# Strided convolution with group norm and GELU, forward and backward: stores of the input gradient in two halves, the first block's leaf C by halves of channels, and a new order for the G1 stage

## The chip, the cores and the metric

One core of a Trainium2 chip runs the whole program in one launch. The metric is the device time of the program in microseconds (us). PE is the matrix engine, PEld its loading of weights, DVE the vector engine, ACT the scalar engine, POOL the general engine, and SP the queue that issues nearly all transfers.

## The reference

```
x [2, 16000, 256], w [31, 256, 256], gn_gamma [256], gn_beta [256], grad_out [2, 7985, 256], all bf16

def _fwd_reference(x, w, gn_gamma, gn_beta):
    s = 2; L = (T - K) // s + 1                       # 7985
    h = sum over i < 31 of einsum('blc,cd->bld', x[:, i:i + s*L:s, :], w[i])
    mu, var = mean and variance of h over l
    h = (h - mu) / sqrt(var + 1e-5) * gn_gamma + gn_beta
    return gelu(h, approximate=True)

def reference(x, w, gn_gamma, gn_beta, grad_out):
    out, vjp = jax.vjp(_fwd_reference, x, w, gn_gamma, gn_beta)
    return out, *vjp(grad_out)                        # out, dx, dw, dgamma, dbeta
```

It is a convolution of stride 2 with 31 taps over 16000 rows of 256 channels, a normalisation of each channel over the rows, and GELU; then the gradients of all four inputs. The kernel returns them as out_0 to out_4; out_1 is the input gradient.

## The kernel before, in words

The three convolutions (forward, input gradient, weight gradient) are fast convolutions in the manner of Karatsuba, nested over the phases of rows and taps. At each of two levels a product of two-part operands is replaced by three products of A (one part), C_ (the other part) and B_ (their sums or differences). A third level is used where `three` or `outer` says so: `f_three_b` computes the product of the sums with difference weights WD or W2D, ACT copies it inside PSUM into the places where it is needed (L778, L1357), and `f_three_ac` adds the other two. The plain form of the same leaf is `f_leaf`: for each of two halves dh of the output channels, it runs over four tap positions q, two parities par and two halves ch of the input channels; an even q is one matmul of 512 columns, an odd q two of 256.

The stages are F0 (forward, batch item 0), F1 (forward, item 1, with GELU of item 0 beside it), G0 (input gradient, blocks 0 to 2 of item 0), G1 (input gradient from block 3 of item 0 to the end) and W (weight gradient). An input gradient block c has two parts pr, each with the three branches B_, A, C_ and their three leaves.

`f_first` (L966) is the very first forward block. It makes the transformed weights on DVE with `w_sub` (L684): W[B_] as W[C_] - W[A] by halves of channels, W[.][B_], and the difference weights WD. Its three leaves are A (plain, in three pieces, so that it can begin with what is loaded), then C_ and B_ by the three-product form, with their own sums `third` (L700). `keep` (L837) takes the B_ leaf out of PSUM when the block is done.

In the input gradient, `e_load` (L1197) fetches two arrays (dy and h) for each half dh of a block, `e_comp` (L1205) turns them into the gradient ahead of the normalisation (L1212, L1214, L1223; on DVE for the blocks in EDVE, on ACT for the others, the last addition always on DVE) and spreads it into the tile ET. From block 0 of item 1 on, both halves share one buffer. `g_sums` builds the sums `first`, `second`, `third` from it (L1283). `g_seed` (L1391) starts the accumulators of two leaves, `g_evac` (L1401) adds a finished leaf to the B_ branch's result and writes it to the tile HO; with the last leaf of a part, it stores HO, the finished block of rows of out_1. There is one HO: the next part writes it again when the store has read it. `dl_turn` transposes the leaves with transfers for the weight gradient.

The order of all instructions is written out by a planner in the kernel itself (`Plan`, L39). Each operation is recorded with its engine, an assumed duration and what it depends on; a kind is made of the stage, the function and its caller (`"G1 load e_load"`). A due time comes from the PE work recorded so far, followed back through the successors:

```
due[i] = end - full - self.lead.get(o["kind"], 0.0) - self.fine.get(o["kind"], {}).get(o["part"], 0.0)
```

`lead` (L53 on) is an offset for a kind, `fine` one for a kind in a part, the number of the block; a larger offset makes the operation due earlier. `listing` (L335) then walks through an assumed run and gives each free engine the ready operation that is due first; PE may look 13 operations ahead. A transfer, and what depends on a transfer, counts as ready later the later it is due. On the chip each engine executes its instructions strictly in the order that comes out.

Of the kernel before, what the change touches and what calls it, by code (L numbers as in the profile page):

```python
# [20 lines left out]
A, B_, C_ = 0, 1, 2  # L21
# [9 lines left out]
def act(n, extra=0.0):  # L31
    return 0.06 + n * 0.00097 + extra
# [6 lines left out]
class Plan:  # L39
# [3 lines left out]
    def __init__(self, tc):  # L43
# [68 lines left out]
            "G0 turn gelu_batch": -12.0,  # L112
            "G0 w_sum load_w2": -53.0,
            "G0 w_sum w2_outer": -11.5,
            "G1 cp e_comp": 13.5,
            "G1 e_comp e_load": 13.5,
            "G1 g_evac last": -0.5,
            "G1 g_mm g_outer": -7.5,
            "G1 g_mm g_three_ac": -9.0,
            "G1 g_mm g_three_b": -30.5,  # L120
            "G1 g_three_b input_grad": -66.0,
            "G1 keep g_seed": -132.0,
            "G1 load dl_turn": 11.0,
            "G1 load e_load": -8.0,
            "G1 load g_evac": 12.0,
            "G1 spread e_comp": -1.5,
            "G1 tt first": -1.0,
            "G1 tt second": -17.0,
            "G1 tt third": -86.5,
            "G1 turn dl_turn": 3.5,  # L130
            "G1 zero e_comp": -8.0,
            "W keep w_keep": -3.0,
            "W keep weight_grad": -12.5,
            "W leaf_d weight_grad": 0.5,
# [83 lines left out]
            "G0 turn dl_turn": {0: -1.0, 1: -2.0, 2: -3.0},  # L218
            "G0 turn gelu_batch": {1: -84.5, 5: -72.0},
            "G0 w_sum load_w2": {3: 79.0},  # L220
            "G1 cp e_comp": {1: 17.0, 2: -24.5},
            "G1 e_comp e_load": {0: 33.5, 2: 1.5, 3: 0.5},
            "G1 g_evac last": {2: 6.5, 3: 5.0},
            "G1 g_mm g_outer": {1: -18.5, 2: -6.0, 3: -2.5},
            "G1 g_mm g_three_ac": {0: -75.0, 1: -51.0, 2: 8.5, 3: -1.5},
            "G1 g_mm g_three_b": {1: -16.5, 2: 16.5, 3: 21.0},
            "G1 g_seed input_grad": {1: -64.5, 2: 8.5, 3: 6.5},
            "G1 keep g_evac": {1: -1.5, 2: -8.0, 3: -5.5},
            "G1 load dl_turn": {0: -3.5, 1: -1.5, 2: 3.5},
            "G1 load e_load": {0: -112.0, 1: -15.0, 2: -56.0, 3: 1.0},  # L230
            "G1 load g_evac": {1: -23.0, 3: -26.0},
            "G1 spread e_comp": {0: -92.5, 1: -85.5, 2: -11.0, 3: -5.5},
            "G1 tt first": {3: -5.0},
            "G1 tt second": {0: -34.0, 1: 7.0, 2: 14.0, 3: 6.0},
            "G1 tt third": {3: 86.5},
            "G1 turn dl_turn": {0: 0.5, 1: 1.5, 2: 0.5, 3: 1.0},
            "G1 zero e_comp": {2: 20.0, 3: 23.0},
            "W keep w_keep": {0: 2.5, 3: -11.5, 4: 11.0, 5: 6.5, 6: -13.0},
            "W keep weight_grad": {0: 7.0, 1: 1.5, 2: -4.0, 3: -2.0, 4: 23.5},
            "W leaf_d weight_grad": {0: 1.5, 1: -14.5, 2: -49.5, 3: 27.0, 4: -0.5, 5: -6.5, 6: -16.0, 7: 12.5, 8: -21.0},  # L240
# [230 lines left out]
def conv_stem_kernel(  # L471
# [20 lines left out]
    HM = 256  # L492
# [32 lines left out]
    def sb(off, *shape, dt=BF16):  # L525
        n = int(np.prod(shape)) * (2 if dt == FP32 else 1)
        assert off % 32 == 0 and off + 2 * n <= AR, (off, shape)
        v = arena[:, off // 2:off // 2 + n]
        if dt == FP32:
            v = v.bitcast(FP32)  # L530
        if len(shape) == 1:
            return v
        names = "abcdefg"[:len(shape)]
        return v.rearrange("p (" + " ".join(names) + ") -> p " + " ".join(names), **dict(zip(names, shape)))
# [7 lines left out]
    def load(out, in_, nbytes, run, eng="SP", slack=None, own=False):  # L542
        if plan.stage in ONE and nbytes > 4096 and not own:
            eng = "SP"
        e = {"SP": nc.sync, "POOL": nc.gpsimd, "ACT": nc.scalar}[eng]
        pk = 8192 if run >= 4096 else 4096 if eng == "POOL" else run
        np_ = nbytes / pk
        ns = (PKS if out.space == bass.MemoryType.DRAM else PK)[pk]
        add(eng, {"POOL": 0.74, "SP": 0.46 + 0.00016 * np_, "ACT": 0.4}[eng], [out], [in_],
            lambda: e.dma_start(out=out, in_=in_), dma=np_ * ns / 16e3 * 1.03, ns=ns, tp=SH[pk], slack=slack)  # L550
# [19 lines left out]
    U = [sb(o, 2, F) for o in (138240, 142592, 205312)]  # L570
# [119 lines left out]
    def i_tap(q, par, br, lf):  # L690
        return 8 * q + par + 4 * (lf == C_) + 2 * (br == C_)
# [70 lines left out]
    def f_three_b(ps, br, lf, op, co, we):  # L762


        jobs = []
        for dh in range(2):
            for q2 in range(2):
                for par in range(2):
                    for ch in range(2):
                        o0 = (2 * par + ch) * XM + co + q2  # L770
                        n = we if q2 + par + ch else HM
                        jobs.append((0, slice(HM * dh, HM * dh + n), WD[br, lf][:, ch, q2, par, dh * P:(dh + 1) * P],
                                     op[:, 1, o0:o0 + n], dh + q2 + par + ch == 0))
        f_mm(ps, jobs, [ps[:, 0]], [WD[br, lf], op[:, 1]])
        for o, i, sc in ((ps[:, 1, 0:HM], ps[:, 0, HM:512], 1.0), (ps[:, 1, HM:512], ps[:, 0, HM:512], -1.0),
                         (ps[:, 0, HM:512], ps[:, 0, 0:HM], -1.0)):
            add("ACT", act(256), [o], [i],
                lambda o=o, i=i, sc=sc: nc.scalar.activation(out=o, in_=i, func=ACT.Copy, scale=sc))  # L778

    def f_three_ac(ps, br, lf, u, co, we, wo):  # L780
        for half, ua, ww in ((0, u[:, 0], we), (1, u[:, 1], wo)):
            for dh in range(2):
                jobs = []
                for q2 in range(2):
                    for par in range(2):
                        for ch in range(2):
                            q = 2 * q2 + half
                            if i_tap(q, par, br, lf) < K:
                                o0 = (2 * par + ch) * XM + co + q2
                                jobs.append((dh, slice(HM * half, HM * half + ww),  # L790
                                             W[br][:, lf, ch, q, par, dh * P:(dh + 1) * P], ua[:, o0:o0 + ww], False))
                f_mm(ps, jobs, [ps[:, dh]], [W[br][:, lf], ua, ps[:, dh]])
# [25 lines left out]
    def flat2(ps):  # L818
        return ps[:].rearrange("p a f -> p (a f)")
# [146 lines left out]
    def f_first(xt):  # L966
        for sl in (A, C_):
            for ch in range(2):
                for v in ([slice(None)] if ch or sl == C_ else [0, 1]):
                    w_sub(*(W[br][:, sl, ch, :, v] for br in (B_, C_, A)))  # L970
        ops, third, second = f_sums(xt, 0, 0, B_, 0, [W[B_][:, A, 0, :, v] for v in range(2)])
        second(A)
        second(C_)
        for br in (B_, A, C_):
            for ch in range(2):
                w_sub(W[br][:, B_, ch], W[br][:, C_, ch], W[br][:, A, ch])
            v = W[br][:, B_]
            w_sub(WD[br, B_], v[:, :, 1:4:2], v[:, :, 0:4:2])
        for br in (A, C_, B_):
            for lf in (A, C_):  # L980
                v = W[br][:, lf]
                w_sub(WD[br, lf], v[:, :, 1:4:2], v[:, :, 0:4:2])
        third(C_, U[2])
        third(B_, U[1])
        pa, pc, pb = ring[0], ring[1], ring[3]
        f_leaf(pa, B_, A, ops[A], 0, HM, HM, True, (0,), (0,))
        f_leaf(pa, B_, A, ops[A], 0, HM, HM, False, (0,), (1,))
        f_leaf(pa, B_, A, ops[A], 0, HM, HM, False, (1,))
        for ps, lf, u in ((pc, C_, U[2]), (pb, B_, U[1])):
            f_three_b(ps, B_, lf, ops[lf], 0, HM)  # L990
            f_three_ac(ps, B_, lf, u, 0, HM, HM)
        tb = TS[A].rearrange("p d f -> p (d f)")
        keep(tb, flat2(pb))
        ve(RB[:, 0], flat2(pa), tb, ALU.add)
        ve(RB[:, 1], flat2(pc), tb, ALU.subtract)
# [397 lines left out]
    def g_evac(b, c, pr, br, lf, ps):  # L1393
        if br == B_:
            keep(GRB[:, 0 if lf == A else 1].rearrange("p e f -> p (e f)"), flat2(ps))
            return
        ho = HO[pr % len(HO)]
        k = (0 if br == A else 1) + (0 if lf == A else 2)
        g = GRB[:, 0 if lf == A else 1]
        add("DVE", dve(1024, 1), [ho[:, :, k, :]], [ps[:], g],  # L1400
            lambda: nc.vector.tensor_tensor(out=ho[:, :, k, :], in0=ps[:], in1=g, op=ALU.add))  # L1401
        if br == C_ and lf == C_:
            n0 = 512 * c + 256 * pr
            r = P if c < 3 or pr == 0 else 104
            load(out_1[b, 8 * n0:8 * n0 + 16 * r, :].rearrange("(p r) c -> p (r c)", r=16),
                 ho[0:r].rearrange("p e k f -> p (e k f)"), r * 8192, 4096, "POOL", slack=60.0)

    G3 = {(b, br, B_) for b in range(NB) for br in ORDER}
    GO = {(b, c) for b, c in ((0, 3), (1, 0), (1, 1), (1, 2), (1, 3))}
# [456 lines left out]
```

## Time and profile before

| | |
|---|---|
| median of 3 runs | 1148.43 us (1147.74 to 1150.5) |
| the profiled execution | 1148.4 us, span 1146.6 us |
| PE busy | 1117.3 us, 97% |
| DVE busy | 998.8 us, 87% |
| ACT, POOL busy | 532.4 us, 124.4 us |
| moved by DMA | 243.57 MB, mean 212 GB/s |
| PE idle ahead of the forward's matmuls (L742) | 12.6 us |
| PE idle ahead of the input gradient's (L1330) | 9.5 us |

In the rows of the profile a group of instructions has its line, engine, operation, output <- input, and the number of executions; then the busy time, the mean duration in ns, and the idle time of the engine ahead of it with what ended it. In a timeline a row has the start, the duration, the engine, the line, the operation, and in brackets the idle time ahead of it. In a table of windows a row has the stretch, its length, the busy time of each engine (PE, PEld, DVE, ACT, POOL) with its instructions, the clock that was granted to PE, the share of DMA and GB/s. In the list of waits: who waited for what, us in total, times, the longest.

### The profile page before, as it was taken

How to read it: one execution, taken by the hardware profiler on the slowest of the kernel's cores; microseconds unless marked ns; L12 is line 12 of the kernel's file. 1: busy time of each engine (PE TensorE's matmuls, PEld its weight loads, DVE VectorE, ACT ScalarE, POOL GpSimd, SP SyncE). 2: the span in 40 equal slices, each digit the busy share in tenths (PEclk: the TensorE clock that was granted, in tenths of full speed). 3: DMA queues.
4: the chain of work that ended last, by engine and by line, in shares of the span. 5: the costliest groups of instructions: out<-in, count | busy, mean ns of one | idle time of the engine just before them, and what ended most of it. 6: DMA issues, size and time to landing. Idle time of an engine off the chain costs nothing. (4 is left out here: it accounts for less than half of the span.)

```text
span 1146.6 us, 18837 instructions
## 1 busy us (share of the span) xinstructions
PE 1117.3 (97%) x7598; PEld 749.3 (65%) x7652; DVE 998.8 (87%) x932; ACT 532.4 (46%) x817; POOL 124.4 (11%) x221
## 2 busy tenths in 40 slices
PE   5999999999999999999999899999999999999998
PEld 3888899877777884444444444444488766666785
DVE  7997787798989998998999777976799998788995
ACT  1254453768777488987744255633212212111200
POOL 0000000000000002231233133232200000000000
PEclk8999999999999999999999999999999999999999
DMA  9476658678895699999989688886998815999564
GB/s 220 66 175 138 164 139 172 147 189 192 193 222 132 192 363 277 280 259 277 229 224 218 136 214 190 205 214 163 247 334 267 291 64 200 350 333 308 185 199 128
DMA packets 345999, 243.57 MB, mean 212 GB/s; under 512 B 233569, under 2 KB 317159, under 8 KB 341735
## 3 DMA queue, kind: packets, MB, share of 16 engines
q1 hardware_dynamic: 338807, 223.47, 73.4%
q0 software_dynamic: 7104, 18.89, 5.8%
q8 instruction: 60, 0.98, 0.4%
q14 instruction: 28, 0.23, 0.1%
HBM read 106.24 MB, written 80.25 MB: 163 GB/s over the span
## 5 line engine op out<-in xcount | busy, mean ns | idle before, releaser
L742 PE MATMUL ps<-arena 128*128 128x256 bf16 (+4 forms) x3460 | 408.4, 282 | 12.6 <-DMA arena<-in_x_dram 6.0
L1330 PE MATMUL ps<-arena 128*128 128x512 bf16 (+1 forms) x1833 | 401.6, 377 | 9.5 <-DVE arena L1283 3.3
L742 PEld LDWEIGHTS <-arena 128*128 128x128 bf16 x3460 | 339.1, 99 | 81.7 <-DMA arena<-in_x_dram 6.3
L1330 PEld LDWEIGHTS <-arena 128*128 128x128 bf16 x1872 | 183.6, 98 | 226.3 <-issue 10.2
L1537 PE MATMUL ps<-arena 128*128 128x256 bf16 (+1 forms) x2305 | 308.3, 296 | 3.4 <-DVE arena L1703 1.8
L1537 PEld LDWEIGHTS <-arena 128*128 128x128 bf16 x2320 | 226.7, 98 | 85.1 <-DVE arena L1607 1.9
L837 ACT ACTIVATE arena<-ps 128x1024 f32<-128x1024 f32 x109 | 110.8, 1021 | 253.1 <-PE ps L1537 82.7
L700 DVE TENSOR_TENSOR arena<-arena 128x2080 bf16<-128x2080 bf16 (+8 forms) x126 | 156.5, 1266 | 34.4 <-PE ps L742 33.8
L550 POOL DMA_DIRECT2D dld<-arena x144 | 104.3, 727 | 259.7 <-DMA arena<-arena 247.3
L1117 DVE TENSOR_TENSOR arena<-arena 128x2048 bf16<-128x2048 bf16 (+1 forms) x80 | 95.6, 1195 | 9.1 <-ACT arena L1109 4.9
L1283 DVE TENSOR_TENSOR arena<-arena 128x1032 bf16<-128x1032 bf16 (+1 forms) x126 | 87.4, 725 | 8.1 <-ACT arena L1232 4.8
L1502 DVE TENSOR_TENSOR arena<-arena 128x4096 bf16<-128x4096 bf16 (+1 forms) x50 | 87.1, 1773 | 5.9 <-DMA arena<-in_x_dram 5.7
L1391 DVE TENSOR_TENSOR ps<-ps,arena 128x2048 f32<-128x2048 f32 x30 | 68.9, 2297 | 24.9 <-PE ps L1330 13.8
L1401 DVE TENSOR_TENSOR arena<-ps,arena 128x1024 bf16<-128x1024 f32 x64 | 77.0, 1218 | 8.0 <-PE ps L1330 5.3
L857 ACT ACTIVATE arena<-ps 128x512 bf16<-128x512 f32 (+1 forms) x64 | 37.1, 581 | 54.0 <-PE ps L742 53.5
L1639 ACT COPY ps<-ps 128x256 f32<-128x256 f32 x54 | 19.3, 358 | 84.2 <-PE ps L1537 82.5
L559 POOL MEMSET arena<- 128x128 bf16 (+11 forms) x40 | 8.6, 245 | 428.3 <-DVE arena L700 139.9
L1357 ACT COPY ps<-ps 128x512 f32<-128x512 f32 x48 | 27.7, 577 | 48.6 <-PE ps L1330 48.4
L1708 DVE TENSOR_TENSOR arena<-arena 128x4608 bf16<-128x4608 bf16 x16 | 40.6, 2551 | 4.7 <-PE ps L1537 4.7
L812 ACT ACTIVATE arena<-ps 128x512 f32<-128x512 f32 x56 | 29.6, 597 | 32.3 <-DVE ps L822 18.8
L778 ACT ACTIVATE ps<-ps 128x256 f32<-128x256 f32 x75 | 27.6, 369 | 35.3 <-PE ps L742 34.1
L1623 DVE TENSOR_TENSOR arena<-arena 128x2048 bf16<-128x2048 bf16 x36 | 42.8, 1219 | 1.4 <-PE ps L1537 1.4
(81 smaller groups left out, 716.5 us busy)
## 6 DMA issues: line engine op xcount, KB each, us to landing
arena<-in_x_dram SPq DMA_DIRECT2D x28, 1024.0 KB
dld<-arena POOLq DMA_DIRECT2D x144, 128.0 KB, 4.0
arena<-hd SPq DMA_DIRECT2D x32, 512.0 KB
out_dram<-arena SPq DMA_DIRECT2D x14, 1024.0 KB
arena<-in_x_dram SPq DMA_DIRECT2D x26, 512.0 KB
arena<-dld SPq DMA_DIRECT2D x18, 640.0 KB
arena<-dld SPq DMA_DIRECT2D x18, 576.0 KB
vl<-arena SPq DMA_DIRECT2D x36, 256.0 KB
```

The source lines that it names most:

```text
L550: lambda: e.dma_start(out=out, in_=in_), dma=np_ * ns / 16e3 * 1.03, ns=ns, tp=SH[pk], slack=slack)
L700: lambda: nc.vector.tensor_tensor(out=o, in0=a, in1=b, op=ALU.add))
L742: yield nc.tensor.matmul(ps[:, dh, cs], lhsT=wt, rhs=mv, start=s0, stop=False, skip_group_check=True)
L837: lambda: nc.scalar.activation(out=out, in_=ps, func=ACT.Copy, scale=scale))
L1117: add("DVE", dve(nf), [o], [a, b_], lambda: V.tensor_tensor(out=o, in0=a, in1=b_, op=op))
L1283: lambda: nc.vector.tensor_tensor(out=o, in0=a, in1=b, op=ALU.subtract))
L1330: yield nc.tensor.matmul(ps[:, e, 0:wide], lhsT=lt, rhs=mv, start=s0, stop=False, skip_group_check=True)
L1391: lambda: nc.vector.tensor_tensor(out=o, in0=x, in1=g, op=ALU.add))
L1401: lambda: nc.vector.tensor_tensor(out=ho[:, :, k, :], in0=ps[:], in1=g, op=ALU.add))
L1502: add("DVE", dve(o.free_size()), [o], [a, b], lambda: nc.vector.tensor_tensor(out=o, in0=a, in1=b, op=ALU.add))
L1537: yield nc.tensor.matmul(ps[:, s, c0:c1], lhsT=lt, rhs=mv, start=s0, stop=False, skip_group_check=True)
L1623: add("DVE", dve(2048), [o], [u, v], lambda o=o, u=u, v=v: nc.vector.tensor_tensor(out=o, in0=u, in1=v, op=ALU.subtract))
```

## The change

Three edits. In `f_first`, leaf C_ is computed by the plain `f_leaf`, in two pieces by halves ch of the input channels, in place of the three-product form; its sum `third(C_, U[2])` goes. In `g_evac`, the store of a finished block of rows is issued as two stores, each for one half of the 4096 columns of a partition's row (4096 bytes per partition in place of 8192). And the offsets of the G1 stage, in `lead` and in `fine`, are replaced.

```diff
@@ Plan.__init__, self.lead @@
-            "G1 cp e_comp": 13.5,
-            "G1 e_comp e_load": 13.5,
-            "G1 g_evac last": -0.5,
-            "G1 g_mm g_outer": -7.5,
-            "G1 g_mm g_three_ac": -9.0,
-            "G1 g_mm g_three_b": -30.5,
-            "G1 g_three_b input_grad": -66.0,
-            "G1 keep g_seed": -132.0,
+            "G1 cp e_comp": 7.0,
+            "G1 e_comp e_load": 12.0,
+            "G1 g_mm g_outer": -15.0,
+            "G1 g_mm g_three_ac": -8.5,
+            "G1 g_mm g_three_b": -35.0,
+            "G1 g_seed input_grad": 8.5,
+            "G1 g_three_b input_grad": -11.0,
+            "G1 keep g_evac": -1.0,
+            "G1 keep g_seed": -108.5,
             "G1 load dl_turn": 11.0,
-            "G1 load e_load": -8.0,
-            "G1 load g_evac": 12.0,
-            "G1 spread e_comp": -1.5,
-            "G1 tt first": -1.0,
-            "G1 tt second": -17.0,
-            "G1 tt third": -86.5,
-            "G1 turn dl_turn": 3.5,
-            "G1 zero e_comp": -8.0,
+            "G1 load e_load": -6.0,
+            "G1 load g_evac": 14.5,
+            "G1 spread e_comp": -5.5,
+            "G1 tt second": -16.0,
+            "G1 tt third": -128.0,
+            "G1 turn dl_turn": 4.0,
+            "G1 zero e_comp": -6.0,
@@ Plan.__init__, self.fine @@
...
-            "G1 e_comp e_load": {0: 33.5, 2: 1.5, 3: 0.5},
+            "G1 e_comp e_load": {0: 43.0, 1: -32.5, 2: 24.0, 3: -0.5},
...
-            "G1 g_seed input_grad": {1: -64.5, 2: 8.5, 3: 6.5},
+            "G1 g_seed input_grad": {0: -1.0, 2: -1.5, 3: 3.5},
...
-            "G1 load e_load": {0: -112.0, 1: -15.0, 2: -56.0, 3: 1.0},
-            "G1 load g_evac": {1: -23.0, 3: -26.0},
-            "G1 spread e_comp": {0: -92.5, 1: -85.5, 2: -11.0, 3: -5.5},
+            "G1 load e_load": {0: -80.0, 1: -15.5, 2: -89.0, 3: 1.0},
+            "G1 load g_evac": {0: -29.0, 1: -33.0, 3: -42.0},
+            "G1 spread e_comp": {0: -90.0, 1: -54.0, 2: -2.0, 3: -2.5},
...
@@ f_first @@
-        third(C_, U[2])
         third(B_, U[1])
         pa, pc, pb = ring[0], ring[1], ring[3]
         f_leaf(pa, B_, A, ops[A], 0, HM, HM, True, (0,), (0,))
         f_leaf(pa, B_, A, ops[A], 0, HM, HM, False, (0,), (1,))
         f_leaf(pa, B_, A, ops[A], 0, HM, HM, False, (1,))
-        for ps, lf, u in ((pc, C_, U[2]), (pb, B_, U[1])):
-            f_three_b(ps, B_, lf, ops[lf], 0, HM)
-            f_three_ac(ps, B_, lf, u, 0, HM, HM)
+        f_leaf(pc, B_, C_, ops[C_], 0, HM, HM, True, (0,))
+        f_leaf(pc, B_, C_, ops[C_], 0, HM, HM, False, (1,))
+        f_three_b(pb, B_, B_, ops[B_], 0, HM)
+        f_three_ac(pb, B_, B_, U[1], 0, HM, HM)
@@ g_evac @@
-            load(out_1[b, 8 * n0:8 * n0 + 16 * r, :].rearrange("(p r) c -> p (r c)", r=16),
-                 ho[0:r].rearrange("p e k f -> p (e k f)"), r * 8192, 4096, "POOL", slack=60.0)
+            for e in range(2):
+                load(out_1[b, 8 * n0:8 * n0 + 16 * r, :].rearrange("(p r) c -> p (r c)", r=16)[:, 2048 * e:2048 * e + 2048],
+                     ho[0:r, e].rearrange("p k f -> p (k f)"), r * 4096, 4096, "POOL", slack=60.0)
```

More of the change, by code (lines that the diff above doesn't have):

```diff
@@ L220, in __init__ @@
             "G0 w_sum load_w2": {3: 79.0},
-            "G1 cp e_comp": {1: 17.0, 2: -24.5},
-            "G1 e_comp e_load": {0: 33.5, 2: 1.5, 3: 0.5},
[L223 to L226, printed above, removed]
-            "G1 g_seed input_grad": {1: -64.5, 2: 8.5, 3: 6.5},
-            "G1 keep g_evac": {1: -1.5, 2: -8.0, 3: -5.5},
-            "G1 load dl_turn": {0: -3.5, 1: -1.5, 2: 3.5},
-            "G1 load e_load": {0: -112.0, 1: -15.0, 2: -56.0, 3: 1.0},
-            "G1 load g_evac": {1: -23.0, 3: -26.0},
-            "G1 spread e_comp": {0: -92.5, 1: -85.5, 2: -11.0, 3: -5.5},
[L233 to L237, printed above, removed]
+            "G1 cp e_comp": {0: 11.0, 1: 20.0, 2: 21.0},
+            "G1 e_comp e_load": {0: 43.0, 1: -32.5, 2: 24.0, 3: -0.5},
+            "G1 g_evac last": {0: 7.5, 1: -1.5, 2: 3.0, 3: 7.5},
+            "G1 g_mm g_outer": {0: 12.0, 1: 3.0, 2: -4.5, 3: 0.5},
+            "G1 g_mm g_three_ac": {0: -161.5, 1: -7.0, 2: 5.5, 3: -1.0},
+            "G1 g_mm g_three_b": {0: 1.0, 1: 11.5, 2: 19.0, 3: 20.0},
+            "G1 g_seed input_grad": {0: -1.0, 2: -1.5, 3: 3.5},
+            "G1 g_three_b input_grad": {0: 14.5, 1: 26.5, 2: -9.5, 3: 6.0},
+            "G1 keep g_evac": {0: -5.5, 1: -112.5, 2: 5.5, 3: -6.5},
+            "G1 keep g_seed": {0: -5.5, 1: 6.0, 2: 21.5, 3: 13.0},
+            "G1 load dl_turn": {0: -3.0, 1: -2.0, 2: 3.5},
+            "G1 load e_load": {0: -80.0, 1: -15.5, 2: -89.0, 3: 1.0},
+            "G1 load g_evac": {0: -29.0, 1: -33.0, 3: -42.0},
+            "G1 spread e_comp": {0: -90.0, 1: -54.0, 2: -2.0, 3: -2.5},
[3 rows of a table added]
+            "G1 turn dl_turn": {0: -3.0, 1: -1.5, 3: 1.0},
+            "G1 zero e_comp": {2: 0.5, 3: 24.5},
             "W keep w_keep": {0: 2.5, 3: -11.5, 4: 11.0, 5: 6.5, 6: -13.0},
```

3 rows, old and new, of the table MIR are left out of this document.

## Prediction

> **What bounds the kernel now.** I read the page, then the waits of PE, its timeline over the start, the windows around its idle stretches, and last the queues of DVE and SP there.
>
> ```profile
> span 1146.6 us, 18837 instructions
> ...
> PE 1117.3 (97%) x7598; PEld 749.3 (65%) x7652; DVE 998.8 (87%) x932; ACT 532.4 (46%) x817; POOL 124.4 (11%) x221
> ...
> L742 PE MATMUL ps<-arena 128*128 128x256 bf16 (+4 forms) x3460 | 408.4, 282 | 12.6 <-DMA arena<-in_x_dram 6.0
> L1330 PE MATMUL ps<-arena 128*128 128x512 bf16 (+1 forms) x1833 | 401.6, 377 | 9.5 <-DVE arena L1283 3.3
> ```
>
> PE is the bound: 1117.3 of 1146.6 us. What can be won is its idle time, 12.6 us in the forward stage (L742) and 9.5 in the input gradient (L1330), and time at a reduced clock. DVE with 87% is close behind. The waits of PE name the pieces:
>
> ```profile
> PE ps L742 <- DMA arena<-in_x_dram: 6.0, 2, 4.7
> PE ps L742 <- DVE arena L684: 4.4, 1, 4.4
> PE ps L1330 <- DVE arena L1283: 3.3, 1, 3.3
> PE ps L742 <- DVE arena L700: 1.9, 1, 1.9
> ```
>
> The second is in the first block, which the change rewrites; the third is in the stage whose order it plans anew. The first and fourth wait for input and first sums, which it leaves alone. The timeline of PE at the start, and windows (us, PE, PEld, DVE, ACT, POOL busy, then clock, DMA share, GB/s) around both waits:
>
> ```profile
> 12.21 6.44 PE L742 MATMUL ps<-arena 128*128 128x512 bf16 x24 [1.88 <-DVE arena L700]
> 23.07 37.15 PE L742 MATMUL ps<-arena 128*128 128x256 bf16 x307 [4.42 <-DVE arena L684]
> ```
> ```profile
> 23.10:27.90 4.80, 4.80 (x21) 3.08 (x22) 4.80 (x5) 1.08 (x3) 0.00 (x0) 0.50 0.92 123
> 60.00:80.00 20.00, 20.00 (x185) 17.86 (x184) 18.42 (x17) 11.53 (x30) 0.00 (x0) 1.00 0.76 212
> 656.50:659.70 3.20, 0.01 (x1) 0.00 (x0) 2.62 (x4) 0.49 (x1) 1.03 (x2) 0.99 0.84 165
> 659.80:663.00 3.20, 3.20 (x8) 1.19 (x9) 1.67 (x2) 2.56 (x5) 1.89 (x4) 0.50 0.83 202
> ```
>
> Each idle stretch has a second price: after 4.42 us idle the clock is 0.50 for 4.8 us, after 3.28 idle it is 0.50 for 3.2. Half of that is lost, 2.4 and 1.6 us. So the stretches cost 6.8 and 4.9 us. A 256-column matmul at full clock costs 20.00/185 = 0.108 us.
>
> The Trainium skill (TensorE: Matmul & The Clock Gate, section "The HAM clock gate") says that the clock halves after an idle window of about 3.4 us. By it a remainder under 3.4 us costs no half clock; by the row here 3.28 was enough. A remainder of 3.3 us would so cost 3.3 by the page and 4.9 by the row; one under 3 us is priced alike by both.
>
> **The first block.** Why did PE wait until 23.07? DVE and ACT there, and DVE's load up to 100 us:
>
> ```profile
> 12.67 3.53 DVE L700 TENSOR_TENSOR arena<-arena 128x2080 bf16<-128x2080 bf16 x3
> 16.12 18.24 DVE L684 TENSOR_TENSOR arena<-arena 128x2048 bf16<-128x2048 bf16 x16
> 34.28 2.33 DVE L700 TENSOR_TENSOR arena<-arena 128x4192 bf16<-128x4192 bf16 x1
> 39.77 1.03 ACT L837 ACTIVATE arena<-ps 128x1024 f32<-128x1024 f32 x1 [4.96 <-PE ps L742]
> ```
> ```profile
> 20.00:30.00 10.00, 6.93 (x37) 4.71 (x38) 10.00 (x10) 1.10 (x3) 0.00 (x0) 0.66 0.84 119
> 30.00:40.00 10.00, 10.00 (x89) 8.54 (x88) 10.00 (x9) 1.34 (x4) 0.00 (x0) 1.00 0.00 0
> 40.00:50.00 10.00, 10.00 (x94) 8.93 (x92) 9.66 (x10) 3.98 (x8) 0.00 (x0) 1.00 0.51 70
> 50.00:60.00 10.00, 10.00 (x94) 8.93 (x92) 9.94 (x7) 3.27 (x7) 0.00 (x0) 1.00 1.01 155
> 80.00:100.00 20.00, 20.00 (x185) 17.86 (x183) 14.78 (x13) 7.23 (x13) 0.00 (x0) 1.00 0.98 159
> ```
>
> The second row is sixteen w_sub of 18.24/16 = 1.14 us. In the order of the kernel before, the third and fourth make the two channel halves of W[B_][C_], the sixth their difference WD, which f_three_b of leaf C needs: 16.12 + 6 x 1.14 = 22.96, and PE starts at 23.07. The plain leaf needs no WD; its first half needs only the third w_sub, its second half the fourth.
>
> Removed: third(C_), one of the three in the first row (3.53/3 = 1.18 us of DVE), three PSUM copies on ACT (idle there, nothing), and 48 matmuls of 256 columns. Added: 16 of 512 and 32 of 256 columns, which is 64 times 256: 16 x 0.108 = 1.7 us more PE. The third w_sub now ends near 16.12 + 3 x 1.14 - 1.18 = 18.4, and PE finishes the first half of leaf A at 12.21 + 6.44 = 18.65. So the gap closes, the clock stays up, and the later pieces follow: the fourth w_sub ends at 19.5, while the first C half takes 32 x 0.108 = 3.5 us. If instead the planner puts leaf A's second half there, it fills the same hole. PE alone gains 4.42 + 2.4 - 1.7 = 5.1 us; the first block, which now ends just before 39.77 (ACT's row), would end near 34.6.
>
> DVE doesn't let all of it through. Its windows are full from 20 to 60 (idle 0.4) and leave 1.58 idle from 60 to 80; from 80 it has 5.2 of 20. WD of C is only postponed, since the next blocks' f_outer reads it; removed is 1.18. So to about 80 us it can deliver 1.18 + 0.4 + 1.58 = 3.1 us earlier. Bounds: 5.1 gained if the planner works further ahead; 1.7 lost if the gap stays. I take 3.1, by the DVE rows. The plan of what follows shifts as a whole and its leads are the same; of the 12.6 us idle of L742 the three waits above are 12.3, so the rest of the forward stage has none to add or lose cheaply, and I put nothing on it.
>
> **The G1 order.** SP's and DVE's timelines ahead of the idle 3.28 us:
>
> ```profile
> 627.85 16.89 SPq L555 DMA_TRANSPOSE arena<-arena  x6
> 644.88 0.46 SPq L550 DMA_DIRECT2D out_dram<-arena  x1
> 645.39 0.35 SPq L550 DMA_DIRECT2D arena<-dyd  x1
> 645.78 1.81 SPq L550 DMA_DIRECT2D arena<-hd  x1
> ```
> ```profile
> 654.32 0.75 DVE L1214 TENSOR_SCALAR arena<-arena,stats 128x2048 bf16<-128x2048 bf16 x1 [1.26 <-DMA arena<-dyd]
> 657.05 0.81 DVE L1212 TENSOR_SCALAR arena<-arena,stats 128x2048 bf16<-128x2048 bf16 x1 [1.98 <-DMA arena<-hd]
> 657.90 1.22 DVE L1223 TENSOR_TENSOR arena<-arena 128x2048 bf16<-128x2048 bf16 x1
> 659.04 0.69 DVE L1283 TENSOR_TENSOR arena<-arena 128x1032 bf16<-128x1032 bf16 x1
> ```
>
> A store of a row block goes out at 644.88, the two e_load halves right behind it, and the second lands only at 657. DVE stands in e_comp (L1214, L1212, L1223) in its fixed order, and behind them is the `second` (L1283) that PE's g_outer needs: PE idles from 656.5 to 659.8. In the planner a smaller lead means a later due time. For part 0 the load's lead was -8 - 112 = -120 and is -6 - 80 = -86; the store's was 12 and is 14.5 - 29 = -14.5. The loads become due 34 us earlier, the store 26 later: the loads should now go out ahead of the store, and a transfer that isn't behind it lands before DVE gets there. That would return all of 3.28 + 1.6 = 4.9 us.
>
> The other leads move too. e_comp of part 1 becomes due 34 us later (13.5 to 12 - 32.5), the loads of part 2 31 us later (-64 to -95), and `second`, `third`, the seeds' and partial sums' leads change by up to tens of us. Any of them can leave a short wait; the nearest row is the first-sum wait of 1.9 us above. I take 1.0 off: 3.9 gained. Bounds: 4.9 gained, or 4.9 lost again if one such stall stands somewhere else besides this one.
>
> **The store halves.** The page's issues of this form, and those around the stall show their price:
>
> ```profile
> out_dram<-arena SPq DMA_DIRECT2D x14, 1024.0 KB
> arena<-hd SPq DMA_DIRECT2D x32, 512.0 KB
> ```
>
> With the last block of each batch item, which is shorter, sixteen stores become 32: 16 more issues of 0.46 us on SP, 7 us over the input gradient, most of it where SP waits for PE or DVE anyway. Both halves wait for the same last g_evac, so nothing starts sooner; what waits for the store is the next write of HO, a branch later. On the path: 0, bounds 0 and 0.46 for each load that stands right behind a store. The bytes are the same.
>
> **Sum.** The profiled execution took 1148.4 us (span 1146.6 plus 1.8 around it), the median of the runs is 1148.43. 1148.4 - 3.1 - 3.9 - 0 = 1141.4.
>
> **Rivals.** (a) First block only: the stall at 656 is cured and an equal one appears in another block of G1, since PE, DVE and ACT hand over within a microsecond there. For: many leads moved at once; against: the one big stall has a cause which the new leads address. 1148.4 - 3.1 = 1145.3.
>
> (b) G1 only: DVE, full from 20 to 60, gives nothing back. For: no idle in those windows; against: PE's wait ended on a w_sub that it no longer needs. 1148.4 - 3.9 = 1144.5.
>
> (c) Slower: the planned issue order puts e_comp in DVE's queue ahead of the landing of its loads in further blocks. Place: DVE's in-order queue in G1, behind SP's stores. Price: 3.28 + 1.6 = 4.9 us each, as now. The old one and two new ones give 9.8 - 3.1 = +6.7: 1155.1. It decides from the point where a load lands over about 3 us after DVE's turn for it. For: the (1, *) blocks have one buffer for the loads, so a late load can't be run ahead of; against: in the other three blocks the row for PE shows no such wait now. The Trainium skill (DMA: Bandwidth & Descriptors, section "Bandwidth") speaks against the halves: it wants transfers of at least 1 MiB, giving 6.15 us for one. By it two halves occupy the queue longer and such a load lands later still; no run here shows it yet.
>
> (d) More than forecast: 5.1 + 4.9 come through, 1138.4, and a little more if the transition to the weight gradient gains as well.
>
> That the change doesn't do what it says is unlikely: the leaf's instructions are fixed in number. Only the order is open.
>
> **Chances.** Forecast 0.60 (own range 1138 to 1144.5), a 0.14, b 0.08, c 0.14, d 0.04. About 0.3% (3.4 us) is what a measurement of this kernel can tell from no change, so faster means under 1145.0: forecast, b and d, 0.72; same is a, 0.14; slower is c, 0.14. The range runs from 1137, d with something over, to 1151, which holds a and a mild c and leaves the rest of c out.
>
> **What would show it.** Right: PE idle before the first block's second group near 0 in place of 4.42, matmuls at clock 1.00 from 23 to 28, the keep (ACT, L837) that ended the block at 39.77 coming 3 to 5 us earlier, and the later blocks of the forward stage about 3 us early. In G1 the loads ahead of the store, no PE wait over 2 us, the clock at 1.00 throughout, and 32 stores of 512 KB and less. Wrong: a new PE wait on w_sub or f_sums (L684, L700) between 25 and 80 us; a DVE wait on arena<-hd or arena<-dyd over 2 us in G1; a longer idle before L1537 when the weight gradient starts.

## The result, and the profile after

| | before | after |
|---|---|---|
| median | 1148.04 us, 20 runs (1143.79 to 1150.81) | 1145.67 us, 20 runs (1143.74 to 1148.86) |
| ratio | 1 | 0.9981 (95%: 0.9972 to 0.9989) |
| profiled execution, span | 1146.6 us | 1144.1 us |

The change gives 2.4 us by the medians and 2.2 by the ratio. It is faster, since the interval lies below 1, but much less so than the 7.0 us forecast, and by the prediction's own line for faster, under 1145.0, it counts as the same: it is the time of rival (a), 1145.3. The lines below are numbered two or three higher after the change (L744 is L742, L1332 is L1330, L1359 is L1357, L1540 is L1537). From the page and PE's waits:

```profile
PE 1120.0 (98%) x7652; PEld 748.4 (65%) x7652; DVE 997.0 (87%) x931; ACT 530.1 (46%) x814; POOL 126.3 (11%) x221
...
L744 PE MATMUL ps<-arena 128*128 128x256 bf16 (+4 forms) x3460 | 407.9, 281 | 10.0 <-DMA arena<-in_x_dram 5.8
L1332 PE MATMUL ps<-arena 128*128 128x512 bf16 x1872 | 403.9, 377 | 7.8 <-ACT ps L1359 4.8
...
out_dram<-arena SPq DMA_DIRECT2D x35, 512.0 KB
```
```profile
PE ps L1332 <- ACT ps L1359: 4.8, 3, 3.1
...
PE ps L744 <- DVE arena L686: 1.0, 1, 1.0
PE ps L744 <- ACT ps L780: 0.9, 1, 0.9
```

The old long waits on DVE (4.4 us at L742, 3.3 at L1330) are both gone. In the forward stage 1.0 and 0.9 stand in place of 4.4. In the input gradient a wait of 3.1 us on ACT stands in place of 3.3 on DVE. The halves of the stores are 512 KB each (28 of the 35 in the row are the halves of fourteen of 1024 KB; seven others had that size before), and 416 KB for the two shorter blocks. PE's timeline at the start, the DVE and ACT rows that bear on it, and windows:

```profile
12.00 9.89 PE L744 MATMUL ps<-arena 128*128 128x512 bf16 x48 [1.88 <-DVE arena L702]
22.85 8.90 PE L744 MATMUL ps<-arena 128*128 128x512 bf16 x64 [0.96 <-DVE arena L686]
32.67 27.54 PE L744 MATMUL ps<-arena 128*128 128x256 bf16 x247 [0.92 <-ACT ps L780]
```
```profile
14.76 18.25 DVE L686 TENSOR_TENSOR arena<-arena 128x2048 bf16<-128x2048 bf16 x16
```
```profile
36.37 1.02 ACT L839 ACTIVATE arena<-ps 128x1024 f32<-128x1024 f32 x1 [3.35 <-PE ps L744]
```
```profile
23.00:28.00 5.00, 5.00 (x36) 3.33 (x35) 5.00 (x5) 0.00 (x0) 0.00 (x0) 1.00 0.77 165
655.00:658.90 3.90, 3.90 (x19) 1.67 (x17) 0.80 (x2) 1.90 (x2) 0.00 (x0) 1.00 1.13 235
658.90:662.00 3.10, 0.05 (x2) 0.02 (x1) 1.01 (x2) 3.10 (x5) 0.00 (x0) 1.00 1.44 141
662.90:666.30 3.40, 3.40 (x10) 1.26 (x9) 2.89 (x2) 2.08 (x4) 3.40 (x6) 0.52 0.79 176
```

The clock is 1.00 where it was 0.50 in the first block, and the keep that ended this block comes at 36.37 in place of 39.77. Near 659 an idle stretch and a half clock behind it are there as before: 3.05 us idle, and some 1.65 us lost in 3.4 us at clock 0.52.

Where the time went, stage by stage: the first matmul of each stage, found by laying the instructions of one profiled execution each beside the planner's list. The last row is taken before rounding.

| us from the span's start | F1 | G0 | G1 | end of G1 | last matmul |
|---|---|---|---|---|---|
| before | 212.9 | 414.6 | 597.7 | 832.0 | 1142.6 |
| after | 209.9 | 411.6 | 593.8 | 828.9 | 1140.1 |
| after less before | -3.1 | -3.1 | -4.0 | -3.2 | -2.5 |

F0 gains 3.1. G0 gains 0.9, G1 loses 0.8, and together they take 417.3 us where they took 417.4: a gain of 0.1 in place of 3.9. The split between these two is not clear of the spread of single executions: with the first block's edit alone, which leaves the order of G0 as it was, G0 took 1.1 us less as well. The weight gradient loses 0.7.

The queues of ACT and SP near the new stall, after the change:

```profile
651.47 0.59 ACT L1359 COPY ps<-ps 128x512 f32<-128x512 f32 x1
657.00 2.19 ACT L1223 ACTIVATE arena<-arena,stats 128x1024 bf16<-128x1024 bf16 x2 [4.94 <-DMA arena<-dyd]
659.10 2.35 ACT L1221 ACTIVATE arena<-arena,stats 128x1024 bf16<-128x1024 bf16 x2
661.36 0.57 ACT L1359 COPY ps<-ps 128x512 f32<-128x512 f32 x1
```
```profile
617.01 0.32 SPq L552 DMA_DIRECT2D arena<-hd  x1
...
620.78 0.71 SPq L552 DMA_DIRECT2D arena<-dyd  x1
...
643.70 0.91 SPq L552 DMA_DIRECT2D out_dram<-arena  x2
644.78 6.05 SPq L557 DMA_TRANSPOSE arena<-arena  x2
650.93 0.53 SPq L552 DMA_DIRECT2D arena<-dyd  x1
651.51 0.42 SPq L552 DMA_DIRECT2D arena<-hd  x1
```

The loads that stood behind the store at 645.4, for block 1 of item 1, now go out at 617.0 and 620.8, ahead of that store (643.70), as forecast. But the loads at 650.9 and 651.5 are those of the block after it, block 2. (The number in the planner's kinds is one lower: a block's loads and e_comp are recorded while the block ahead of it is worked on, so that part 0 is block 1, and part 1 is block 2.) SP spends 6.05 us on two transposes, the loads go out at 650.9 and 651.5, the first lands near 657, ACT stands idle 4.94 us in e_comp for it (L1223), and the copy that PE needs (L1359) is queued behind four e_comp instructions, until 661.36. It is the old stall on another engine, one block later.

### The profile page after: what moved, and what is told of

The parts are those of the page before. It is cut to its first block, busy times and chain, and to the rows that moved or that the text cites. A ratio compares the mean times of both kernels' runs of the same rounds, so it can differ in the third digit from the quotient of the medians.

```text
span 1144.1 us, 18907 instructions
## 1 busy us (share of the span) xinstructions
PE 1120.0 (98%) x7652; PEld 748.4 (65%) x7652; DVE 997.0 (87%) x931; ACT 530.1 (46%) x814; POOL 126.3 (11%) x221
## 4 chain that ended last, share of the span: by engine, by line
PE 78%; DVE 12%; DMA 3%; issue 3%; ACT 2%; SPq 2%; DVEq 0%; ACTq 0%
PE ps L744 32%; PE ps L1540 25%; PE ps L1332 21%; DVE ps L1393 2%; DVE arena L1403 2%; SPq L552 1%; DVE arena L1285 1%; DVE arena L1119 1%; DVE arena L686 1%; DVE arena L702 1%; DVE arena L1225 1%; SPq L557 1%; DMA arena<-vl 1%; DMA arena<-in_x_dram 1%; DMA arena<-dyd 1%
## 5 line engine op out<-in xcount | busy, mean ns | idle before, releaser
L744 PE MATMUL ps<-arena 128*128 128x256 bf16 (+4 forms) x3460 | 407.9, 281 | 10.0 <-DMA arena<-in_x_dram 5.8
L1332 PE MATMUL ps<-arena 128*128 128x512 bf16 x1872 | 403.9, 377 | 7.8 <-ACT ps L1359 4.8
L744 PEld LDWEIGHTS <-arena 128*128 128x128 bf16 x3460 | 338.0, 98 | 79.8 <-DMA arena<-in_x_dram 6.1
L1332 PEld LDWEIGHTS <-arena 128*128 128x128 bf16 x1872 | 183.6, 98 | 227.3 <-issue 15.5
L1540 PE MATMUL ps<-arena 128*128 128x256 bf16 (+1 forms) x2320 | 308.9, 296 | 2.4 <-DVE arena L1706 1.5
L1540 PEld LDWEIGHTS <-arena 128*128 128x128 bf16 x2320 | 226.8, 98 | 84.5 <-issue 1.9
L702 DVE TENSOR_TENSOR arena<-arena 128x2064 bf16<-128x2064 bf16 (+8 forms) x125 | 155.4, 1268 | 31.9 <-PE ps L744 31.4
L1359 ACT COPY ps<-ps 128x512 f32<-128x512 f32 x48 | 27.8, 580 | 41.7 <-PE ps L1332 41.7
```

Source lines behind the costliest of these rows:

```text
L702: lambda: nc.vector.tensor_tensor(out=o, in0=a, in1=b, op=ALU.add))
L744: yield nc.tensor.matmul(ps[:, dh, cs], lhsT=wt, rhs=mv, start=s0, stop=False, skip_group_check=True)
L1332: yield nc.tensor.matmul(ps[:, e, 0:wide], lhsT=lt, rhs=mv, start=s0, stop=False, skip_group_check=True)
L1540: yield nc.tensor.matmul(ps[:, s, c0:c1], lhsT=lt, rhs=mv, start=s0, stop=False, skip_group_check=True)
```

## The experiments

All were timed beside the kernel before. The ratios are to it, with 95% intervals; a gain in us is worked out from the ratio, which pairs the runs, and so differs by about 1 us at most from the difference of the medians. "Theory" at first: the first block brought its 3.1 us, and the store and G1 edits together gave nothing, since one stall was exchanged for another.

**The first block's edit alone** (the `f_first` part of the diff; the order of every later stage stays as before).

> The kernel before with the first block's edit alone; the order of every later stage is the same as before. Theory (the first block brought 3.1 us, and the store and G1 edits together cost about 0.7): 3.1 us faster than before, PE idle ahead of the first block's later groups about 2 us in place of 4.4, and the idle 3.28 us with half clock behind it near 653 still there. Rival 1 (the halves of the store cost about what the new order won): the same. Rival 2 (the first block's gain is lost again on the way, and G1 brought the rest): under 1.5 us faster.

1146.70 us against 1147.99, ratio 0.9987 (0.9974 to 1.0000): 1.5 us. The interval holds 3.0 but not 3.1, and also rival 1 (none). Its trace has the waits that were expected, and the one near 653 is there:

```profile
PE ps L1330 <- DVE arena L1283: 3.3, 1, 3.3
PE ps L742 <- DVE arena L684: 2.3, 2, 2.1
```

The traces give a better measure of F0. The first matmul of F1 comes at 211.1 to 212.9 in the six profiled executions without the edit (mean 212.1) and at 209.0 to 210.0 in the six with it (mean 209.7). So the traces put the edit at 2.4 us of F0; the 3.1 of the first pair of traces had some luck in it. The interval of the timed gain, 0 to 3.0 us, holds 2.4; no run shows why its middle, 1.5, is smaller still.

**The kernel before with two loads moved.** They go out near 632 in place of 645, ahead of three transposes and the store. Only the emission order is changed: two operations, named by kind, part and number, go to a place before (0) or behind (1) a third one.

```diff
+MOVES = [
+    ([('G1 load e_load', 0, 0), ('G1 load e_load', 0, 1)], 0, ('G1 turn dl_turn', 0, 0)),
+]
...
```

> The kernel before with one move in SP's queue alone: the two e_load transfers that stood behind the store at 644.88 go out ahead of the three transposes before it, near 632. Theory (PE's idle 3.28 us came from DVE standing in e_comp for that transfer, and is worth 4.9 us with the half clock): 4 to 5 us faster, no idle of PE over 1 us between 640 and 680. Rival 2 (PE, DVE and ACT hand over so closely in G1 that another wait takes its place): 0 to 1.5 us faster, with a wait of 2 us or more somewhere behind.

1144.20 us, ratio 0.9957 (0.9942 to 0.9972): 4.9 us, as expected by the theory. Lines are 15 higher in this kernel. DVE's queue and PE's timeline:

```profile
653.77 0.74 DVE L1229 TENSOR_SCALAR arena<-arena,stats 128x2048 bf16<-128x2048 bf16 x1
654.43 0.81 DVE L1227 TENSOR_SCALAR arena<-arena,stats 128x2048 bf16<-128x2048 bf16 x1
655.28 1.22 DVE L1238 TENSOR_TENSOR arena<-arena 128x2048 bf16<-128x2048 bf16 x1
656.42 0.69 DVE L1298 TENSOR_TENSOR arena<-arena 128x1032 bf16<-128x1032 bf16 x1
```
```profile
639.71 40.56 PE L1345 MATMUL ps<-arena 128*128 128x512 bf16 x187
```

No wait on DMA in DVE's queue, and PE runs 40 us without a gap. So the cause that the prediction read from the trace and the price it put on it were right; this one move is worth about twice the whole change.

**The changed kernel with ACT's work moved back.** The four e_comp of the late block stand behind the copy and the keep, DVE's addition behind the seed.

> The changed kernel with one move alone: ACT's four e_comp of the next block stand behind the copy of f_three_b's counterpart g_three_b and the seed's keep, not ahead of them, and DVE's addition behind the seed. Theory (the changed kernel's idle 3.05 us near 659 is ACT standing in e_comp for a late load with the copy queued behind it, worth 3.05 + 1.65 us): 3 to 4.7 us faster than the changed kernel, 5.4 to 7.1 faster than before. Rival 1 (the halves delay everything in the queue): under 1 us faster than the changed kernel. Rival 2 (another wait takes its place): the same.

1147.32 us, ratio 0.9989 (0.9979 to 0.9999): not faster than the changed kernel. Theory failed here, rival 2 was right. The lines are 16 higher:

```profile
655.96 0.57 ACT L1375 COPY ps<-ps 128x512 f32<-128x512 f32 x1 [5.18 <-PE ps L1348]
656.44 1.03 ACT L855 ACTIVATE arena<-ps 128x1024 f32<-128x1024 f32 x1
657.36 2.19 ACT L1239 ACTIVATE arena<-arena,stats 128x1024 bf16<-128x1024 bf16 x2
659.44 2.37 ACT L1237 ACTIVATE arena<-arena,stats 128x1024 bf16<-128x1024 bf16 x2
663.15 2.18 ACT L1250 COPY arena<-arena 128x768 bf16<-128x768 bf16 x4 [1.34 <-DVE arena L1241]
665.23 1.01 ACT L855 ACTIVATE arena<-ps 128x1024 f32<-128x1024 f32 x1
```
```profile
668.63 11.72 PE L1348 MATMUL ps<-arena 128*128 128x512 bf16 x47 [4.07 <-DVE ps L1409]
```

The copy comes in time, at 655.96. But e_comp and its spreads (L1250) now occupy ACT until 665.3, the next keep (L855) waits behind them, the seed on DVE (L1409) behind that, and PE idles 4.07 us. That left two readings: the load is late, or ACT has too much to do here.

**The changed kernel with its stores whole**, in its own order: the first half's place takes the whole store, the second's nothing.

> The changed kernel in its own order, but each store of a row block goes out whole at the place of its first half and nothing at the place of the second. Theory: the halves cost nothing on the path, so the time is that of the changed kernel within 0.5 us, and PE's idle near 659 stays within 0.5 us of 3.05. Rival 1 (sixteen more issues and smaller transfers cost what the order won): 2 to 4 us faster than the changed kernel, the idle near 659 under 1 us.

1146.13 us, ratio 0.9977 (0.9969 to 0.9986), the changed kernel 0.9981. The same, and the stall is there with 3.38 us:

```profile
662.15 6.11 PE L1332 MATMUL ps<-arena 128*128 128x512 bf16 x15 [3.38 <-ACT ps L1359]
```

With the order held fixed the halves cost and bring nothing that can be measured. Rival 1 is out.

**The changed kernel with two transposes behind the late loads.**

```diff
+MOVES = [
+    ([('G1 turn dl_turn', 0, 6), ('G1 turn dl_turn', 0, 7)], 1, ('G1 load e_load', 1, 1)),
+]
...
```

> The changed kernel with one move in SP's queue alone: the two e_load transfers of block 2 (issued at 650.9 and 651.5) go out ahead of the two transposes that kept SP from 644.8 to 650.8. Moving ACT's work back (the run before) only moved the wait, so the theory now is that the late transfer itself is the cause: with it landing some 4 us earlier, ACT is through with e_comp before PE needs the copy. Then 3 to 4.7 us faster than the changed kernel, about 1141 to 1142.7, and no idle of PE over 1 us between 640 and 690. Rival 2 (ACT's four e_comp of 1.1 us and the spreads fill G1 here wherever they stand): a wait of 2 us or more stays within 30 us of the place, and the time is that of the changed kernel within 1 us.

1142.17 us against 1147.40, ratio 0.9952 (0.9938 to 0.9966). Against the changed kernel's 0.9981 that is 0.9971, 3.3 us, at the lower end of what the theory expected; the two intervals, 0.9938 to 0.9966 and 0.9972 to 0.9989, don't touch. Lines are 15 higher:

```profile
645.38 0.35 SPq L567 DMA_DIRECT2D arena<-dyd  x1
645.78 1.80 SPq L567 DMA_DIRECT2D arena<-hd  x1
```
```profile
653.63 2.19 ACT L1238 ACTIVATE arena<-arena,stats 128x1024 bf16<-128x1024 bf16 x2 [2.46 <-DMA arena<-dyd]
655.73 2.36 ACT L1236 ACTIVATE arena<-arena,stats 128x1024 bf16<-128x1024 bf16 x2
657.99 0.57 ACT L1374 COPY ps<-ps 128x512 f32<-128x512 f32 x1
```
```profile
658.62 19.15 PE L1347 MATMUL ps<-arena 128*128 128x512 bf16 x86 [0.57 <-ACT ps L1374]
```

The loads go out some 5.6 us earlier, ACT is through with e_comp by 658, and PE's idle 3.05 is 0.57. The same ACT work stands in the same place. So the late load was the cause, not the amount of ACT's work.

**The kernel before with the first block's edit and the two loads moved.**

> The kernel before with the first block's edit and the one move of two e_load transfers ahead of three transposes. Theory (both costs are separate and add up): 1.5 + 4.9 to 3.1 + 4.9 = 6.4 to 8.0 us faster than before, 1140 to 1141.6, so faster than before and than the changed kernel. Rival (an earlier start of G1 meets another order of transfers and loses one of the two): under 5.5 us faster.

1141.35 us against 1147.40, ratio 0.9945 (0.9931 to 0.9958): 6.3 us, 0.1 under the lower end of the theory. This version beats both kernels. It is close to the 1141.4 that was forecast for the change, by the two reasons of the forecast, but with an order that does what the forecast believed the new offsets to do. With 4.9 us for the loads, it leaves 1.4 for the first block, near the 1.5 timed for that alone.

**Each of the other two edits alone**: the new offsets, and the halves with the old offsets.

> The kernel before with the new offsets of G1 alone, the first block and the whole stores as before. The planner makes of them an order of its own, 29 of 265 matrix operations of G1 otherwise than in the changed kernel. Theory (the new offsets bring the loads of the next block forward into a place where they come late for ACT): PE's wait on DVE (L1283) near 656 gone, a wait on ACT's copy (L1357) of 2 us or more in its place, the time within 1.5 us of before. Rival (the new offsets are worth the forecast 3.9 and the halves take it): 3 us faster or more.

> The kernel before with the stores in halves alone and the old offsets of G1. Sixteen more operations in the planner's list change its order in G0, G1 and W too (47 of 265 matrix operations of G1). Theory (the halves themselves cost nothing; the order that they cause was fitted to nothing): between 1 us faster and 6 us slower, with the difference in waits of PE that stand at other places than before, none of them behind the second half of a store. Rival 1 (the halves cost by themselves): 2 to 4 us slower, with waits for loads behind second halves.

1193.41 us, ratio 1.0394 (1.0377 to 1.0411), and 1190.96, ratio 1.0377 (1.0363 to 1.0392). Neither was near what any theory expected. The waits of PE that are new and large in the first of them (L1539 is L1537) are in the weight gradient, which neither edit touches:

```profile
PE ps L1539 <- DVE arena L1609: 12.9, 2, 7.6
...
PE ps L1539 <- DVE ps L824: 5.1, 1, 5.1
PE ps L1539 <- DVE ps L1649: 5.0, 2, 2.5
...
PE ps L1539 <- DVE arena L1605: 4.0, 2, 3.6
```

From the last matmul of G1 to the last of all it takes 351.9 us with the new offsets alone and 336.9 with the halves alone, 310.5 before. What the planner's lists show of it: of 206 operations of DVE in the weight gradient, each edit alone moves over 50 (56 and 59), both together (the changed kernel) move 3.

**The same two with the weight gradient in the order of the kernel before.** The list of that stage is written into the kernel:

```diff
-        for i in self.order():
+        seq = self.order()
+        ws = [i for i, o in enumerate(self.ops) if o["kind"].startswith("W ")]
+        inw = set(ws)
+        it = iter([ws[k] for k in WORDER])
+        for i in [next(it) if i in inw else i for i in seq]:
```

> The run with G1's new offsets alone (1193 us), but with the weight gradient's operations in the order that they have in the kernel before; all else, the end of G1 too, as in that run. Theory (its 45 us are the weight gradient's order, which the planner made from another end of G1 and which its offsets don't fit): back to within 5 us of before, with the weight gradient from the first to the last matmul within 3 us of the 310.5 us that lie between 832.0 and 1142.6 in the kernel before. Rival (the late transfers at the end of G1 do it, whatever the order behind): still 30 us or more slower than before.

> The run with the stores in halves and the old offsets (1191 us), but with the weight gradient's operations in the order of the kernel before. Theory: the weight gradient is back within 4 us of before's; what remains is the 11 us that G0 and G1 lost in that run (842.6 in place of 832.0 at the end of G1), so 1156 to 1162. Rival: still 30 us or more slower than before.

1154.78 us against 1146.81, ratio 1.0071 (1.0050 to 1.0092), and 1160.80, ratio 1.0115 (1.0092 to 1.0138). The weight gradient is back at 311.9 and 313.2 us, as expected, so its order was the cause of most of the loss. The first total misses its 5 us by 3: G1 itself, from 597.0 to 837.4, takes 240.4 us with the new offsets alone, 6 more than before's 234.3, which the earlier trace (596.4 to 834.9) had shown by 4 already. With the halves alone it takes 244.6. Together the two take 235.1. In this planner either edit without the other is much worse than none, and the two together are not.

## Why the prediction was right or wrong

**The bound and the two stalls: right.** PE stayed the bound, and both idle stretches were where the time was. The 4.9 us on the one near 656 was measured by the two moved loads: 4.9, with an interval of 3.2 to 6.7.

**First block: right in what it wins, with luck in the size.** The forecast was 3.1; the pair of traces gives 3.1, twelve traces 2.4, the timed runs of this edit alone 1.5 (0 to 3.0). The gap of 4.42 became 0.96 and 0.92, and no half clock follows. But what kept the gain under the 5.1 of PE alone was not the bound by DVE's idle time: behind 22.85 no matmul of the forward stages waits for DVE, and 5.1 less the two waits that are left, 0.96 and 0.92, is 3.2. (In the six traces with the edit the first of the two is 1.0 to 2.1 us long, which leaves 2.1 to 3.2.) That the bound gives nearly the same number is luck. The two waits came about so: the planner put leaf A's second half first and leaf C's first w_sub seventh in DVE's row of sixteen (third before), so that it ended only at 14.76 + 7 x 1.14 = 22.7 and PE waited for it; and with no other matmuls between, ACT's three copies of leaf B_ are no longer covered (0.92). The prediction had put ACT's copies at nothing for the leaf that loses them, and didn't ask what had covered the others.

**The store halves: right** at 0 for the stores, with the order held: the comparison at fixed order shows no cost of 512 KB against 1 MB here, 0.9981 and 0.9977. Rival (c) had expected a longer queue from the halves by the batch rule of the Trainium skill (DMA: Bandwidth & Descriptors, section "Bandwidth": transfers of at least 1 MiB); this case does not show one.

**G1: wrong, and this is nearly the whole miss.** The old stall did go, in the way described, and was worth its 4.9 us. The step that failed is the term behind it, for all that the other offsets could do: "I take 1.0 off: 3.9 gained." It measured 4.7: a stall of 3.05 + 1.65 us came back. The prediction had read the offsets one at a time: e_comp of part 1, the one of block 2, "becomes due 34 us later", so it was expected to come later. It came 25 us earlier, at 657 in place of 682. The last readers of the buffer that the blocks of item 1 share, ACT's spreads of block 1, first before (with e_comp of block 2 behind them), then after:

```profile
679.79 0.70 ACT L1232 COPY arena<-arena 128x256 bf16<-128x256 bf16 x2
...
682.03 2.37 ACT L1219 ACTIVATE arena<-arena,stats 128x1024 bf16<-128x1024 bf16 x2
```
```profile
644.06 2.18 ACT L1234 COPY arena<-arena 128x768 bf16<-128x768 bf16 x4 [1.31 <-DVE arena L1225]
```

What holds the loads of block 2 is not their due time (their own offset hardly changed, -23 to -21.5) but this one buffer. Moving block 1 forward by some 30 us freed it near 646 in place of 680, and the loads of block 2 came next, in the place where two transposes held SP for 6 us. So G0 and G1 together gained 0.1 in place of 3.9, which with the 0.7 lost in the weight gradient is the 4.5 us between the forecast of 7.0 and the 2.5 of the traces. Rival (a) described this, and priced it within 0.4 us of the result, but got 0.14 since "the one big stall has a cause which the new leads address": addressing a stall's cause by an earlier load says nothing of the load behind it in the same buffer.

**The plan of other stages: missed.** "The plan of what follows shifts as a whole" held for the first block's edit: no operation after F0 changes its place. It was not asked of the other two edits, and there it decides: alone they cost 41 and 26 us in a stage that they don't touch. Rival (c) looked for the danger in G1's queue, at 6.7 us; the true one, with one of the two edits alone, was up to six times as large, in the weight gradient, and the pair of edits avoids it by leaving that stage's order almost as it was.

## What to carry to other kernels

When a load is brought forward in a chain through one buffer, follow the chain: ask where the next load in that buffer lands, and which engine stands waiting for it with what queued behind. Move the late transfer itself: moving the work that waited for it only moved the wait (the run with ACT's work moved back), and two transfers moved by hand did more than a new set of offsets for a whole stage. Where a planner writes the order, an edit's largest effect can be the order of a stage that it doesn't touch, so compare the lists of all stages, and measure an edit with the order held fixed as well.

## What the runs showed of the hardware

The half clock does not need an idle stretch of 3 us. Ahead of the weight gradient PE idles 1.5 to 1.8 us in each kernel. The same place in the kernel before and in the first block's edit alone:

```profile
840.56:843.97 3.41, 1.97 (x17) 1.38 (x15) 3.41 (x4) 2.05 (x2) 0.00 (x0) 1.00 1.06 408
844.60:847.90 3.30, 3.30 (x31) 2.95 (x31) 3.30 (x4) 0.00 (x0) 0.00 (x0) 1.00 1.03 395
```
```profile
837.52:840.93 3.41, 1.39 (x13) 0.85 (x11) 3.41 (x4) 1.44 (x2) 0.00 (x0) 1.00 1.03 411
839.00:840.80 1.80, 0.02 (x1) 0.10 (x1) 1.80 (x3) 0.24 (x1) 0.00 (x0) 1.00 1.05 432
840.90:844.20 3.30, 3.30 (x17) 2.37 (x17) 3.30 (x4) 0.00 (x0) 0.00 (x0) 0.50 1.04 381
```

Before, the clock stays at 1.00 behind it; in the other it is 0.50 for 3.3 us, worth 1.7 us by chance. The prediction had priced remainders under 3 us without it, by its one row and by the Trainium skill (TensorE: Matmul & The Clock Gate, section "The HAM clock gate": an idle window of about 3.4 us); here 1.8 us was enough in one execution and not in another.

What differs is where the idle time falls. In each trace every half clock ahead of the program's end is 3.41 us long, or a multiple of it, and all start on one grid of that step (659.65 us is a point of it before, 840.93 in the other). The first row of each view is the step of the grid that holds the 1.8 us: PE was busy for 1.97 of 3.41 us where the clock stayed, and for 1.39 where it fell. Over the twelve traces, from 14 us on and with the clock at 1.00, it fell after each of the 24 steps with PE busy for 0.42 of it or less, and after none of some 3900 with 0.47 or more; of the five in between two were followed by a fall. Behind the first block's gap, in the kernels without that block's edit, the half clock was one or two such steps long (3.4 or 6.8 us). That may be one reason why edits worth 2 us need many runs; that the spread between runs comes from it was not tested.
